# First batch's attention scores from float32 words of K and Q, V loaded behind them, and a new order of the work

## The chip, the cores and the metric

One core of one Trainium2 chip runs the kernel. The metric is device microseconds of one execution, from the first to the last instruction and what lies around them. Engines are named as in the profile: PE is TensorE (PEld its weight loads), DVE is VectorE, ACT is ScalarE, POOL is GpSimd, SP issues the DMAs.

## What is computed

Attention over 4 batches of 8 heads with 576 positions of 64 numbers, in which only scores within `tau` of the row's maximum count, and behind it two feed-forward stages (512 to 2048 to 512) on the 2304 rows that result:

```python
scores = (q @ k.T) / 8
scores = where(scores >= max(scores) - tau, scores, -1e9)
attn = exp(scores - max(scores)); attn /= sum(attn) + 1e-9
x = attn @ v                       # 2304 x 512
h = x @ w_in;  x = (h * tanh(softplus(h))) @ w_out
h = x @ w2_in; out = (h * clip(h + 3, 0, 6) / 6) @ w2_out
```

Inputs and output are float32.

## The kernel before

**Stages.** Attention comes first, and the first product of stage one (`inner`, `gemm1`, line 661) is laid into its gaps. Then come the second product of stage one (`gemm2`, line 825) and both products of stage two (lines 661 and 837). Weights are converted from float32 pairs to two float16 parts each (`convert`, lines 387 to 529); the first matrix is converted during the first batch.

**Attention.** A batch has 4 pairs of heads. A pair has 4 query tiles of 128 positions, each with two heads, and one joined tail tile that holds the last 64 positions of both heads, so 9 head tiles; a batch has 36 and all have 144. For a head tile `scores` (line 1058) fills one of two score buffers in PSUM. Then come the maximum (`peak`, line 1067, DVE), the threshold (line 1072, ACT), the exponential (line 1077, ACT), the mask (line 1080, DVE), the rounding to float16 (line 1085, ACT), its remainder (line 330, `p_ph`, POOL), a DMA transpose of both heads (line 1093, SP) and the product with V (line 1106, PE). V is scaled by one factor a batch, which needs the maxima of all four V blocks (line 937), and is split into a float16 part and a remainder (lines 1013 and 1016).

**K and Q.** The score of a float32 pair is made of rounded parts. The host stacks each transposed head twice, so K and Q have 128 partitions, of which the lower 64 repeat the upper. `pair` loads both (`rk`, `rq`, line 1000, one buffer each). K is scaled and rounded to `kd` on ACT (line 992) and its remainder goes to `kld` on DVE (line 995). Q is rounded to `qs` on ACT (line 985), and on half of the partitions the remainder of Q takes the place of the rounded value, in two subtractions, one for each head (`q_lo`, line 330 with the tile `qs`, POOL or DVE). One product over 128 partitions then adds two of the four partial products, and the two products with `kd` and `kld` give all:

```python
terms = [(st, kd.tile[:, j]), (st, kld.tile[:, j])]
for half in range(2):
    for m, (lh, rh) in enumerate(terms):
        mm(s[j].tile[:, half, :HALF], lh, rh[:, half * HALF : (half + 1) * HALF], ...)
```

That is 4 matmuls of 288 columns for a head, 8 for the tail, 40 for a pair.

**What sets the order.** A planner (`Plan`) lays the work out when the program is built. Each piece has costs by engine, a due time (from a clock of 2.55 us a head tile, with offsets by kind) and buffers; the planner always takes the piece with the earliest start, and among near ones the earliest due. The constants at the top of the file are its costs and due times. On the chip each engine runs its list in that order and waits on semaphores, so a late operand holds back all that stands behind it. `PIECE` is the number of matmuls of line 661 in one piece (4), `MOE_LAG` how late these are due, and `CONV_STEP` the spacing of the weight conversions.

Of the kernel before, what the change touches and what calls it, by code (L numbers as in the profile page):

```python
# [8 lines left out]
F32 = mybir.dt.float32  # L9
F32R = mybir.dt.float32r  # L10
# [11 lines left out]
P = 128  # L22
# [20 lines left out]
START = 7.2  # L43
PV_OFF = 6.17
PREP_AHEAD = 2.45
CONV_STEP = 1.5
CONV_AT = 3.0
LATE_STEP = 4.0
OUT_STEP = 1.5
OUT_AT = 0.0  # L50
V_AHEAD = 4.0
MOE_OFF = 9.75
MOE_LAG = 8.26
RATE = 1.32
NX = 3
FLIP = 1.61
ALPHA = {"act": 3.07, "pe": 10.98}
FITS = 0.09
# [10 lines left out]
VECTOR = 0.17  # L69
PIECE = 4  # L70
LAG = 4
# [4 lines left out]
NBLK_EARLY = 2 * B - 1  # L76
EASE = {"mk": -1.41, "ph": 1.68, "pl": -3.92, "tr": -1.06, "ex": 0.6, "s": -3.68, "th": -5.15}
# [4 lines left out]
WINDOW = {"pe": 0.05, "dve": 0.05, "act": 0.02, "pool": 0.15, "sp": 0.22}  # L82

# [201 lines left out]
def fused_kernel(ctx: ExitStack, tc, q, k, v, tau, w1i, w1o, w2i, w2o, out):  # L285
# [40 lines left out]
    def ring(name, pool, count, shape, dtype=F32):  # L326
        return Ring(name, maker(pool, name, shape, dtype), count)
# [351 lines left out]
    def inner(blk, early, at=None, gap=0.0):  # L679
# [19 lines left out]
        for fp in range(NG):  # L699
# [14 lines left out]
            if fp % 2:  # L714

                def put(e, he=he, fp=fp):
                    nc.sync.dma_start(out=hd[blk][:, fp // 2], in_=he.tile)

                h_stored[blk, fp // 2] = task(
                    {"sp": 0.5}, put, taken, [he], f"s{fp}", 2.0, fp + VECTOR  # L720
                )
# [183 lines left out]
    r_xts = ring("xts", ap, 1, [P, TAIL])  # L905
    vts, xtail, qts = [], [], []
    for i in range(4):
        pool = ap if i < 2 else ep
        qt = pool.tile([P, 2, QW], F32R, name=f"qs{i}")
        nc.gpsimd.memset(qt[:, 0, S:].bitcast(F32), 0.0)  # L910
        qts.append(qt)
# [7 lines left out]
    r_qs = [Ring("qs", lambda i, name, k=k: qts[2 * k + i], 2) for k in range(2)]  # L919
    r_vh = [Ring("vh", lambda i, name, k=k: vts[2 * k + i], 2) for k in range(2)]  # L920
# [5 lines left out]
    def batch_values(b, begin):  # L926
# [44 lines left out]
    def pair(n, begin, values, sets):  # L971
        b, hp = n // NPAIR, n % NPAIR
        base = START + begin * STEP
        early = base - PREP_AHEAD * STEP
# [4 lines left out]
        rq, rk = Buf(r_rq), Buf(r_rk)
        qs, kd, kld = Buf(r_qs[sets]), Buf(r_kd[sets]), Buf(r_kld[sets])  # L980
        vbs, vs, scaled = values
# [23 lines left out]
        ql = []
        kh = prep({"act": 1.2}, k_hi, [lk], [rk, kd], "kh")
        a = prep({"act": 1.155}, lambda e: q_hi(slice(0, 2)), [lq], [rq, qs], "qh")
        for j in range(2):
            ql.append(prep(both(S), lambda e, j=j: q_lo(e, j), [a], [rq, qs], f"ql{j}_"))
        kl = prep({"dve": 1.42}, k_lo, [kh], [rk, kd, kld], "kl")  # L1010

# [14 lines left out]
        def query_tiles(t, c, o, i):  # L1026
# [118 lines left out]
            for js in whole(MERGE_LO):  # L1145
# [262 lines left out]
```

## Time and profile before

| | |
|---|---|
| Median of 3 runs | 1089.45 us (1085.86 to 1089.76) |
| The profiled execution, its own time | 1089.44 us |
| Its span | 1087.7 us |
| PE busy | 968.7 us, 89% |
| PEld busy | 784.4 us, 72% |
| DVE busy | 604.3 us, 56% |
| ACT busy | 605.1 us, 56% |
| POOL busy | 469.2 us, 43% |
| Mean granted TensorE clock | 0.958 |

The shares are means over stages with different limits: DVE, ACT and POOL do most of their work in the first 700 us, and PE is close to full only behind the first 500. The chain of work that ended last gives PE 71% and DMA 11%, of which the transposes are 9%.

### The profile page before, as it was taken

The numbers are of one execution on the slowest core, as the hardware profiler recorded it, in microseconds if no ns is written. First come the engines' busy times: TensorE is split into PE (matmuls) and PEld (weight loads), VectorE is DVE, ScalarE is ACT, GpSimd is POOL, SyncE is SP. The second block draws the span as 40 slices with busy tenths as digits, with TensorE's granted clock in tenths as the row PEclk, the third lists the DMA queues.
The fourth block names the chain that finished last, engine by engine and source line by source line (L and its number), as shares of the span: only waits on it lengthen the run. The fifth ranks groups of instructions, "written<-read, shape, count | busy, mean of one in ns | idle before, by whom it ended". The sixth has DMA issues, their size and how long they took to land.

```text
span 1087.7 us, 21597 instructions
## 1 busy us (share of the span) xinstructions
PE 968.7 (89%) x8839; PEld 784.4 (72%) x8839; DVE 604.3 (56%) x1068; ACT 605.1 (56%) x982; POOL 469.2 (43%) x408
## 2 busy tenths in 40 slices
PE   2447688898999986979999999999999999999997
PEld 1436577787899875868888888886666667666663
DVE  7778997777787779757679678621211111111110
ACT  6637777787788778546676559522322322223322
POOL 3859766466565658634433025512222222222221
PEclk9856789998999998999999999999999999999999
DMA  6867679999999898966576967410100100100001
GB/s 258 209 172 175 139 191 238 221 229 252 195 219 218 179 227 171 239 236 235 192 233 231 335 230 265 140 40 1 58 29 11 40 30 11 40 20 20 20 1 39
DMA packets 199394, 162.87 MB, mean 150 GB/s; under 512 B 174080, under 2 KB 174080, under 8 KB 194176
## 3 DMA queue, kind: packets, MB, share of 16 engines
q1 hardware_dynamic: 199296, 161.51, 55.7%
q8 instruction: 69, 1.13, 0.4%
q14 instruction: 29, 0.24, 0.1%
HBM read 90.18 MB, written 28.84 MB: 109 GB/s over the span
## 4 chain that ended last, share of the span: by engine, by line
PE 71%; DMA 11%; DVE 8%; POOL 4%; ACT 3%; issue 2%; SPq 0%; ACTq 0%; POOLq 0%; DVEq 0%
PE h_g L661 19%; PE y_y L825 17%; PE y_y L837 17%; DMA pt_tr<-p_ph 9%; PE hp_g L661 9%; PE s_s L1058 4%; PE aux_pv L1106 4%; DVE e_ex L1080 2%; POOL p_ph L330 2%; DVE nm_pk L1067 1%; POOL qs L330 1%; DMA v_lv<-in_v 1%; ACT e_ex L1077 1%; DMA rq_lq<-in_q 1%; DMA raw_lr<-in_moe_w_in 1%
## 5 line engine op out<-in xcount | busy, mean ns | idle before, releaser
L661 PEld LDWEIGHTS <-w 128*128 128x128 f16 x3456 | 333.5, 98 | 66.9 <-issue 5.8
L330 POOL TENSOR_TENSOR p_ph<-e_ex,p_ph 128x128 f16<-128x128 f32 (+3 forms) x160 | 195.2, 1242 | 110.3 <-ACT p_ph L1085 69.0
L330 POOL TENSOR_TENSOR gs_h<-hl_r,gs_h 128x512 f16<-128x512 f32 x72 | 83.5, 1159 | 286.2 <-ACT gs_h L800 286.2
L837 PE MATMUL y_y<-w,gs_h 128*128 128x512 f16 x864 | 201.7, 379 | 0.0
L825 PE MATMUL y_y<-gs_h,w 128*128 128x256 f16 x1728 | 191.7, 273 | 0.0
L661 PE MATMUL h_g<-x_fl,w 128*128 128x256 f16 x1536 | 187.6, 275 | 3.2 <-ACT he_t L709 2.4
L825 PEld LDWEIGHTS <-w 128*128 128x128 f16 x1728 | 168.4, 98 | 19.3
L837 PEld LDWEIGHTS <-gs_h 128*128 128x128 f16 x864 | 84.5, 98 | 82.0
L800 ACT ACTIVATE gs_h<-hl_r 128x512 f16<-128x512 f32 x72 | 45.3, 629 | 172.0 <-PE y_y L837 155.4
L1067 DVE TENSOR_REDUCE nm_pk<-s_s 128x1 f32<-128x576 f32 x144 | 105.8, 751 | 35.3 <-PE s_s L1058 34.4
L1080 DVE SCALAR_TENSOR_TENSOR e_ex<-s_s,thr_th,e_ex 128x576 f32<-128x576 f32 x144 | 111.6, 810 | 15.0 <-ACT thr_th L1072 11.1
L1106 PE MATMUL aux_pv<-vh,pt_tr 128*128 128x65 f16 (+1 forms) x1296 | 91.1, 207 | 29.8 <-DMA pt_tr<-p_ph 28.1
L1077 ACT ACTIVATE e_ex<-s_s,nm_pk 128x576 f32<-128x576 f32 x144 | 104.1, 732 | 18.4 <-DVE nm_pk L1067 16.3
L784 DVE SCALAR_TENSOR_TENSOR hl_r<-hl_r,f,h_g 128x512 f32<-128x512 f32 x36 | 26.9, 747 | 156.2 <-ACT hl_r L778 156.2
L1106 PEld LDWEIGHTS <-pt_tr 128*128 128x128 f16 x2016 | 83.8, 105 | 37.6 <-DMA pt_tr<-p_ph 33.3
L1085 ACT ACTIVATE p_ph<-e_ex 128x576 f16<-128x576 f32 x144 | 95.6, 680 | 25.7 <-DVE e_ex L1080 18.6
L784 DVE SCALAR_TENSOR_TENSOR hl_r<-hl_r,f,hp_g 128x512 f32<-128x512 f32 x36 | 26.9, 746 | 145.3 <-ACT hl_r L778 145.3
L661 PE MATMUL h_g<-xl_x,w 128*128 128x256 f16 x864 | 104.3, 273 | 0.0
L661 PE MATMUL hp_g<-xl_x,w 128*128 128x256 f16 x864 | 103.0, 273 | 0.0
L1058 PE MATMUL s_s<-kda_kh,qs 128*128 128x288 f32 x200 | 68.5, 357 | 26.8 <-DVE e_ex L1080 18.3
L1058 PEld LDWEIGHTS s_s<-kda_kh,qs 128*128 128x128 f32 x200 | 43.2, 216 | 37.0 <-POOL qs L330 14.9
L804 DVE SCALAR_TENSOR_TENSOR gs_h<-hp_e,fscales,gs_h 128x512 f16<-128x512 f32 x72 | 52.6, 744 | 25.8 <-ACT gs_h L798 25.6
(321 smaller groups left out, 1297.0 us busy)
## 6 DMA issues: line engine op xcount, KB each, us to landing
hd<-he_t SPq DMA_DIRECT2D x36, 512.0 KB, 3.3
hl_l<-hd SPq DMA_DIRECT2D x36, 512.0 KB, 4.5
raw_lr<-in_moe_w_in SPq DMA_DIRECT2D x16, 1024.0 KB, 5.5
raw_lr<-in_moe_w_out SPq DMA_DIRECT2D x16, 1024.0 KB, 6.6
rk_lk<-in_k SPq DMA_DIRECT2D x16, 576.0 KB, 5.2
rq_lq<-in_q SPq DMA_DIRECT2D x16, 576.0 KB, 5.1
raw_lw<-in_moe_w_out SPq DMA_DIRECT2D x8, 1024.0 KB, 7.3
v_lv<-in_v SPq DMA_DIRECT2D x16, 320.0 KB, 4.6
```

What stands on the lines that cost most here:

```text
L330: engine[e].tensor_tensor(dst, a, b, ALU.subtract)
L661: mm(hv[:, j, :], wj[:, wl, c * P : (c + 1) * P], x.tile[:, c, xl, :], start=j == 0 and n == 0, stop=j == 1 and n == 11, skip_group_check= ...
L784: nc.vector.scalar_tensor_tensor(half(g), half(g), wsc[2]["f"][:, fp : fp + 1], h.tile, ALU.min, ALU.mult)
L804: nc.vector.scalar_tensor_tensor(s.tile[:, 1], gv(), fs[:, fp : fp + 1], s.tile[:, 0], ALU.mult, ALU.subtract)
L825: mm(yv[:, h, :], wt[m2][f // 2][:, f % 2, wl, c * P : (c + 1) * P], gs[fp].tile[:, gl, f % 2, :], start=fp == 0 and n == 0, stop=fp == NG ...
L837: mm(y.tile[:, j], gs[fp].tile[:, gl, f % 2, j * P : (j + 1) * P], wt[m2][f // 2][:, f % 2, wl, :], start=fp == 0 and n == 0, stop=fp == N ...
L1058: mm(s[j].tile[:, half, :HALF], lh, rh[:, half * HALF : (half + 1) * HALF], start=m == 0, stop=m == len(terms) - 1,)
L1067: nc.vector.tensor_reduce(neg.tile[:, j : j + 1], sv(j), AX.XY, ALU.max, negate=True)
L1077: nc.scalar.activation(ev(j), sv(j), AF.Exp, bias=neg.tile[:, j : j + 1])
L1080: nc.vector.scalar_tensor_tensor(ev(j), sv(j), thr.tile[:, j : j + 1], ev(j), ALU.is_ge, ALU.mult)
L1085: nc.scalar.activation(p16.tile[:, js, :S], e_.tile[:, js], AF.Copy)
L1106: mm(ov[:, dst, :d], pt.tile[:, j, ch, :], part.tile[:, src, vc, :], start=i == j == ch == 0 and part is vh, stop=j == w - 1 and ch == 8, ...
```

## The change

For the batches below `DIRECT`, that is for the first alone, K and Q are no longer split. The upper 64 partitions of each, thus each word once, are loaded straight into the buffers `kd` and `qs` (no `rk`, `rq`, `kld`), ACT scales K in place, and the scores are float32 matmuls over 64 partitions: 2 for a head, 4 for the tail, 20 for a pair. The loads of the first batch may start earlier (`DIRECT_AHEAD`), and its V is due later (`V_FIRST`), behind K and Q of two pairs. The zeros behind `qs` are now filled for each pair on POOL (`pad`) and not once for each buffer. The planner's constants are new, so the whole order is: of its costs and due times the diff shows those that are spoken of later.

```diff
-CONV_STEP = 1.5
+CONV_STEP = 2.06
-MOE_LAG = 8.26
+MOE_LAG = 15.8
-PIECE = 4
+PIECE = 2
...
+        first = START + (begin - V_FIRST) * STEP if b == 0 else at
-            a = task({"sp": 0.5}, load, [], [vb], f"lv{i}_", 0.91, 0.0, [prev[5]])
+            a = task({"sp": 0.5}, load, [], [vb], f"lv{i}_", 0.91, first - at, [prev[5]])
...
+        direct = b < DIRECT
-        early = base - PREP_AHEAD * STEP
+        early = base - (DIRECT_AHEAD if direct else PREP_AHEAD) * STEP
...
+        def words(t):
+            return t.tile[:D, :, :S].bitcast(F32)
+
+        def load_words_of(dst, src):
+            return lambda e: nc.sync.dma_start(out=words(dst), in_=src[n][:D])
+
+        def k_scaled(e):
+            nc.scalar.activation(words(kd), words(kd), AF.Copy, scale=qscale[:D])
+
+        def pad(e):
+            nc.gpsimd.memset(qs.tile[:, 0, S:].bitcast(F32), 0.0)
+
+        padded = prep({"pool": 0.16}, pad, [], [qs], "qp")
+        if direct:
+            lk = prep({"sp": 0.5}, load_words_of(kd, k), [], [kd], "lk", 0.82, order=[prev[4]])
+            lq = prep({"sp": 0.5}, load_words_of(qs, q), [], [qs], "lq", 0.82, order=[lk])
+            kl = prep({"act": 1.2}, k_scaled, [lk], [kd], "kh")
+            ql = [lq, lq]
+        else:
...
+                if direct:
+                    qt, ks = qs.tile[:D].bitcast(F32), [kd.tile[:D].bitcast(F32)]
+                else:
+                    qt, ks = qs.tile, [kd.tile, kld.tile]
                 if c < NQ:
                     q0 = j * TAIL + c * P
-                    st = qs.tile[:, j, q0 : q0 + P]
-                    terms = [(st, kd.tile[:, j]), (st, kld.tile[:, j])]
+                    terms = [(qt[:, j, q0 : q0 + P], k[:, j]) for k in ks]
```

In the new order the matmuls of line 661 are laid out differently against the head tiles. Ahead of the 37th, the 73rd and the 109th head tile's scores there stood 84, 544 and 916 of them, and 1256 ahead of the last product with V; now there stand 48, 466, 822 and 1270. The order itself is shown at three places.

The start of SP's list of DMAs, before and then changed (`lv` is V, `lk` and `lq` are K and Q, `lr` is a block of weights):

```order
L954 DMA v_lv_0_0_163<-in_v 128x640
L954 DMA v_lv_0_0_165<-in_v 128x640
L954 DMA v_lv_0_0_167<-in_v 128x640
L954 DMA v_lv_0_0_169<-in_v 128x640
L1000 DMA rk_lk_0_171<-in_k 128x1152
L1000 DMA rq_lq_0_173<-in_q 128x1152
L450 DMA raw_lr_0_0_175<-in_moe_w_in 128x1024
L450 DMA raw_lr_1_0_177<-in_moe_w_in 128x1024
L1000 DMA rk_lk_0_202<-in_k 128x1152
```

```order
L1011 DMA kda_lk_0_159<-in_k 64x1152
L1011 DMA qsa_qp_0_155<-in_q 64x2x576
L1011 DMA kda_lk_0_166<-in_k 64x1152
L1011 DMA qsa_qp_0_157<-in_q 64x2x576
L957 DMA v_lv_0_0_169<-in_v 128x640
L957 DMA v_lv_0_0_171<-in_v 128x640
L957 DMA v_lv_0_0_173<-in_v 128x640
L957 DMA v_lv_0_0_175<-in_v 128x640
L1011 DMA kdb_lk_0_178<-in_k 64x1152
L1011 DMA qsb_qp_0_161<-in_q 64x2x576
L455 DMA raw_lr_0_0_181<-in_moe_w_in 128x1024
```

The four V blocks stood first and one pair's K and Q behind them. Now K and Q of two pairs, on 64 partitions, stand first, V behind them, and K and Q of the other two pairs next.

DVE's list from its first V maximum to its first masks, before and then changed (`vm` is a V maximum, `kl` a K remainder, `vl` a V remainder, `top` a weight maximum, `pk` a score maximum, `e_ex` a mask):

```order
L937 TENSOR_REDUCE vt_vm_0_1_179<-v_lv_0_0_167 128x1
L937 TENSOR_REDUCE vt_vm_0_1_179<-v_lv_0_0_169 128x1
L942 TENSOR_REDUCE vs_ve_1_184<-vt_vm_0_1_179 128x1
...
L995 SCALAR_TENSOR_TENSOR klda_kl_2_197<-rk_lk_0_171,qscale,kda_kh_1_189 128x1152
L1016 SCALAR_TENSOR_TENSOR vla_vl_3_205<-v_lv_0_0_163,vs_ve_1_184,vh_128 128x640
L387 TENSOR_REDUCE top_146<-raw_lr_0_0_175 128x1
L1067 TENSOR_REDUCE nm_pk_0_0_1_218<-s_s_0_0_0_208 128x1
...
L1016 SCALAR_TENSOR_TENSOR vla_vl_3_230<-v_lv_0_0_165,vs_ve_1_184,vh_132 128x640
L1067 TENSOR_REDUCE nm_pk_0_0_1_218<-s_s_0_1_0_220 128x1
L387 TENSOR_REDUCE top_146<-raw_lr_1_0_177 128x1
L1080 SCALAR_TENSOR_TENSOR e_ex_0_0_2_228<-s_s_0_0_0_208,thr_th_0_0_1_240,e_ex_0_0_2_228 128x576
```

```order
L939 TENSOR_REDUCE vt_vm_0_1_195<-v_lv_0_0_169 128x1
L1094 TENSOR_REDUCE nm_pk_0_0_1_201<-s_s_0_0_0_183 128x1
L939 TENSOR_REDUCE vt_vm_0_1_195<-v_lv_0_0_171 128x1
L939 TENSOR_REDUCE vt_vm_0_1_195<-v_lv_0_0_173 128x1
L939 TENSOR_REDUCE vt_vm_0_1_195<-v_lv_0_0_175 128x1
L1094 TENSOR_REDUCE nm_pk_0_0_1_201<-s_s_0_1_0_192 128x1
L944 TENSOR_REDUCE vs_ve_1_210<-vt_vm_0_1_195 128x1
L945 TENSOR_SCALAR vs_ve_1_210<-vs_ve_1_210 128x1
L1107 SCALAR_TENSOR_TENSOR e_ex_0_0_2_204<-s_s_0_0_0_183,thr_th_0_0_1_213,e_ex_0_0_2_204 128x576
```

The first score maximum stood behind all V maxima, the V scale, a K remainder and a V remainder; now it stands behind one V maximum, and the second score maximum stands behind all four.

POOL's list from its first work on the first batch, before and then changed (`qs` is a subtraction into Q, `p_ph` the remainder of the probabilities, `cvt` and `w` are steps of the weight conversion):

```order
L330 TENSOR_TENSOR qs_126<-rq_lq_0_173,qs_126 64x576 x2
L330 TENSOR_TENSOR qs_130<-rq_lq_0_225,qs_130 64x576
L330 TENSOR_TENSOR p_ph_0_0_1_247<-e_ex_0_0_2_228,p_ph_0_0_1_247 128x2x64
L330 TENSOR_TENSOR p_ph_0_0_1_247<-e_ex_0_0_2_228,p_ph_0_0_1_247 128x2x512
L330 TENSOR_TENSOR qs_130<-rq_lq_0_225,qs_130 64x576
L330 TENSOR_TENSOR p_ph_1_0_1_290<-e_ex_1_0_2_269,p_ph_1_0_1_290 128x2x64
L330 TENSOR_TENSOR p_ph_1_0_1_290<-e_ex_1_0_2_269,p_ph_1_0_1_290 128x2x512
L511 TENSOR_TENSOR cvt_c_0__1_281<-cvt_c_0__1_281,eight 128x512 x2
```

```order
L335 TENSOR_TENSOR p_ph_0_0_1_220<-e_ex_0_0_2_204,p_ph_0_0_1_220 128x2x64
L335 TENSOR_TENSOR p_ph_0_0_1_220<-e_ex_0_0_2_204,p_ph_0_0_1_220 128x2x512
L335 TENSOR_TENSOR p_ph_1_0_1_263<-e_ex_1_0_2_241,p_ph_1_0_1_263 128x2x64
L335 TENSOR_TENSOR p_ph_1_0_1_263<-e_ex_1_0_2_241,p_ph_1_0_1_263 128x2x512
L516 TENSOR_TENSOR cvt_c_0__1_288<-cvt_c_0__1_288,eight 128x512 x2
L335 TENSOR_TENSOR p_ph_0_0_1_335<-e_ex_0_0_2_286,p_ph_0_0_1_335 128x2x64
```

The subtractions into `qs` stood among the remainders of the probabilities; in the first batch there are none now, and the list goes from one `p_ph` to the next with only weight steps between.

## Rows read from the trace of the kernel before

**Rows 1.** Windows: stretch, length, busy PE PEld DVE ACT POOL, clock, DMA share, GB/s
```profile
0.00:14.90 14.90, 1.59 (x5) 1.09 (x5) 8.92 (x20) 6.88 (x8) 4.50 (x18) 1.00 0.84 317
14.90:148.50 133.60, 77.05 (x663) 65.89 (x664) 115.23 (x195) 86.36 (x140) 94.59 (x77) 0.74 0.68 174
148.50:253.80 105.30, 93.74 (x1179) 85.74 (x1178) 80.25 (x139) 82.72 (x148) 67.38 (x54) 1.00 1.08 229
253.80:347.00 93.20, 87.94 (x1083) 80.84 (x1081) 73.76 (x134) 76.77 (x141) 55.17 (x47) 0.96 1.03 218
347.00:455.00 108.00, 89.48 (x1103) 80.33 (x1102) 85.19 (x157) 80.94 (x144) 72.61 (x60) 0.95 0.93 199
...
500.00:1087.70 587.70, 581.68 (x4493) 438.67 (x4491) 211.63 (x362) 247.74 (x368) 155.37 (x138) 1.00 0.29 99
```

**Rows 2.** Windows, score maxima alone (line 1067), DVE busy (count)
```profile
14.90:148.50 133.60, 26.34 (x36) 0.74 0.68 174
148.50:253.80 105.30, 26.13 (x37) 1.00 1.08 229
```

**Rows 3.** Windows, first products of the stages alone (line 661), PE, PEld (count)
```profile
14.90:148.50 133.60, 11.99 (x86) 8.67 (x87) 0.74 0.68 174
148.50:253.80 105.30, 55.75 (x460) 42.66 (x458) 1.00 1.08 229
...
347.00:455.00 108.00, 41.36 (x341) 31.56 (x340) 0.95 0.93 199
```

**Rows 4.** Timeline of the opening: start us, us, engine, line
```profile
5.06 1.61 DVE L937 TENSOR_REDUCE vt_vm<-v_lv 128x1 f32<-128x640 f32 x2 [0.40 <-DMA v_lv<-in_v]
6.90 1.60 DVE L937 TENSOR_REDUCE vt_vm<-v_lv 128x1 f32<-128x640 f32 x2 [0.22 <-DMA v_lv<-in_v]
...
13.30 0.61 PE L1058 MATMUL s_s<-kda_kh,qs 128*128 128x288 f32 x1 [3.60 <-POOL qs L330]
...
16.65 0.76 DVE L1067 TENSOR_REDUCE nm_pk<-s_s 128x1 f32<-128x576 f32 x1
...
18.45 1.53 DVE L1080 SCALAR_TENSOR_TENSOR e_ex<-s_s,thr_th,e_ex 128x576 f32<-128x576 f32 x2
```

**Rows 5.** Waits of the first 150 us: us in total, times, longest
```profile
PE s_s L1058 <- POOL qs L330: 7.0, 4, 3.6
...
DVE nm_pk L1067 <- PE s_s L1058: 5.7, 10, 1.6
...
PE s_s L1058 <- DVE kldb_kl L995: 3.3, 1, 3.3
```

**Rows 6.** Lines by form: count, busy us, mean ns, idle before
```profile
L995 DVE SCALAR_TENSOR_TENSOR klda_kl<-rk_lk,qscale,kda_kh 128x1152 fp32r<-128x1152 f32 x10 | 14.3, 1427 | 0.3 <-ACT kda_kh L992 0.3
...
L992 ACT ACTIVATE kda_kh<-rk_lk,qscale 128x1152 fp32r<-128x1152 f32 x10 | 12.5, 1248 | 0.3 <-PE s_s L1058 0.2
...
L330 POOL TENSOR_TENSOR qs<-rq_lq,qs 64x576 fp32r<-64x576 f32 x32 | 46.9, 1466 | 27.5 <-ACT qs L985 26.2
```

**Rows 7.** Windows: score maxima at 40 us, all engines at the batch's end
```profile
40.00:70.00 30.00, 3.01 (x4) 0.67 0.70 178
...
100.00:148.50 48.50, 35.26 (x322) 30.19 (x319) 44.60 (x76) 33.79 (x61) 34.90 (x31) 0.79 0.64 157
```

**Rows 8.** Timeline, score matmuls at the half and the full clock
```profile
48.44 0.44 PE L1058 MATMUL s_s<-kldb_kl,qs 128*128 128x288 f32 x1
...
49.88 0.44 PE L1058 MATMUL s_s<-kldb_kl,qs 128*128 128x288 f32 x1
...
209.63 0.30 PE L1058 MATMUL s_s<-klda_kl,qs 128*128 128x288 f32 x1
...
210.96 0.29 PE L1058 MATMUL s_s<-klda_kl,qs 128*128 128x288 f32 x1
```

**Rows 9.** Float32 matmuls of lines 1227 and 1221: duration ns, min, median, max
```profile
L1227 PE MATMUL aux_fl<-istack,xtail x32: 217/275/323, 116.0 to 456.4; 128*128 128x64 f32 x32
...
L1221 PE MATMUL aux_fl<-ident,xn_dn x64: 270/273/474, 39.5 to 453.7; 128*128 128x128 f32 x64
```

More of the change, by code (lines that the diff above doesn't have):

```diff
@@ L43 @@
 START = 7.2
-PV_OFF = 6.17
+PV_OFF = 3.72
+V_FIRST = 1.0
+DIRECT_AHEAD = 8.0
+DIRECT = 1
 PREP_AHEAD = 2.45
-CONV_STEP = 1.5
+CONV_STEP = 2.06
 CONV_AT = 3.0
-LATE_STEP = 4.0
-OUT_STEP = 1.5
+LATE_STEP = 2.61
+OUT_STEP = 2.39
 OUT_AT = 0.0
-V_AHEAD = 4.0
+V_AHEAD = 6.29
 MOE_OFF = 9.75
-MOE_LAG = 8.26
+MOE_LAG = 15.8
 RATE = 1.32
@@ L56 @@
 FLIP = 1.61
[L57 removed]
+ALPHA = {"act": 3.07, "pe": 6.71}
 FITS = 0.09
@@ L69 @@
 VECTOR = 0.17
-PIECE = 4
+PIECE = 2
+TR_DMA = 1.22
+HD_DMA = 1.6
 LAG = 4
@@ L719, in inner @@
                 h_stored[blk, fp // 2] = task(
-                    {"sp": 0.5}, put, taken, [he], f"s{fp}", 2.0, fp + VECTOR
+                    {"sp": 0.5}, put, taken, [he], f"s{fp}", HD_DMA, fp + VECTOR
                 )
@@ L890, in fused_kernel @@
     r_rk = ring("rk", ap, 1, [P, 2, S])
+    r_qs = [ring("qs" + "ab"[k], (ap, ep)[k], 2, [P, 2, QW], F32R) for k in range(2)]
     r_kd = [ring("kd" + "ab"[k], (ap, ep)[k], 2, [P, 2, S], F32R) for k in range(2)]
@@ L905, in fused_kernel @@
     r_xts = ring("xts", ap, 1, [P, TAIL])
-    vts, xtail, qts = [], [], []
+    vts, xtail = [], []
     for i in range(4):
         pool = ap if i < 2 else ep
-        qt = pool.tile([P, 2, QW], F32R, name=f"qs{i}")
-        nc.gpsimd.memset(qt[:, 0, S:].bitcast(F32), 0.0)
-        qts.append(qt)
         vt = pool.tile([P, 2, NQ + 1, D + 1], F16, name=f"vh{i}")
@@ L973, in pair @@
         base = START + begin * STEP
[L974 removed]
+        direct = b < DIRECT
+        early = base - (DIRECT_AHEAD if direct else PREP_AHEAD) * STEP
         def prep(engines, fn, deps, bufs, tag, dma=0.0, at=early, order=()):
             return add(engines, fn, deps, bufs, at, 0.0, dma, f"{tag}{n}", order)
[L979 to L980 removed]
+        qs, kd = Buf(r_qs[sets]), Buf(r_kd[sets])
+        if not direct:
+            rq, rk, kld = Buf(r_rq), Buf(r_rk), Buf(r_kld[sets])
         vbs, vs, scaled = values
@@ L1000, in load @@
             return lambda e: nc.sync.dma_start(out=dst.tile, in_=src[n])
-        lk = prep({"sp": 0.5}, load(rk, k), [], [rk], "lk", 1.64, order=[prev[4]])
-        lq = prep({"sp": 0.5}, load(rq, q), [], [rq], "lq", 1.64, order=[lk])
-        prev[4] = lq
[L1005 to L1010, printed above, removed]
+        def words(t):
[13 more added lines that the diff above has]
+        else:
+            lk = prep({"sp": 0.5}, load(rk, k), [], [rk], "lk", 1.64, order=[prev[4]])
+            lq = prep({"sp": 0.5}, load(rq, q), [], [rq], "lq", 1.64, order=[lk])
+            ql = []
+            kh = prep({"act": 1.2}, k_hi, [lk], [rk, kd], "kh")
+            a = prep({"act": 1.155}, lambda e: q_hi(slice(0, 2)), [lq], [rq, qs], "qh")
+            for j in range(2):
+                ql.append(prep(both(S), lambda e, j=j: q_lo(e, j), [a], [rq, qs], f"ql{j}_"))
+            kl = prep({"dve": 1.42}, k_lo, [kh], [rk, kd, kld], "kl")
+        prev[4] = lq
         def v_hi(e):
@@ L1044, in scores @@
             def scores(j):
+                if direct:
+                    qt, ks = qs.tile[:D].bitcast(F32), [kd.tile[:D].bitcast(F32)]
+                else:
+                    qt, ks = qs.tile, [kd.tile, kld.tile]
                 if c < NQ:
                     q0 = j * TAIL + c * P
-                    st = qs.tile[:, j, q0 : q0 + P]
-                    terms = [(st, kd.tile[:, j]), (st, kld.tile[:, j])]
+                    terms = [(qt[:, j, q0 : q0 + P], k[:, j]) for k in ks]
                 else:
-                    flat = qs.tile.rearrange("p a n -> p (a n)")
+                    flat = qt.rearrange("p a n -> p (a n)")
                     terms = [
-                        (flat[:, q0 : q0 + P], k.tile[:, jj])
+                        (flat[:, q0 : q0 + P], k[:, jj])
                         for jj, q0 in enumerate((FULL, S))
-                        for k in (kd, kld)
+                        for k in ks
                     ]
@@ L1116, in query_tiles @@
             for j in heads:
-                deps = [ql[j], kl] if c < NQ else [*ql, kl]
-                held = [s[j], qs, kd, kld]
+                deps = [ql[j], kl] if c < NQ else [*ql, kl, padded]
+                held = [s[j], qs, kd] if direct else [s[j], qs, kd, kld]
+                cost = (0.56, 0.96) if c < NQ else (1.08, 1.92)
                 a = go(
-                    {"pe": 0.56 if c < NQ else 1.08}, lambda e, j=j: scores(j), deps + [prev[0]],
+                    {"pe": cost[direct]}, lambda e, j=j: scores(j), deps + [prev[0]],
                     held, "s", j,
```

7 lines of the change are left out of this document (3 added, 4 removed).

## The prediction

> **What bounds the kernel now.** I read the busy time by stretch first [rows 1]. From 500 us to the end TensorE is busy 581.68 of 587.70 us, with the clock at 1.00: that stage is pure matrix work and its length is the work that is left over. Everything before it is attention, with the first product of the expert stage (line 661) pushed into TensorE's gaps; there no engine is full. So the end of the kernel is the time at which attention is over plus the matrix work not yet done by then. The sums below are therefore about the length of attention, and about matmuls that move across its end.
>
> Within attention the first batch stands out. The row maxima (line 1067) number 36 a batch, one for each tile of one head (and one for each joined tail) [rows 2]: the first 36 take 133.60 us, 3.71 us each, and the next 37 take 105.30 us, 2.85 each. In those 133.60 us VectorE is busy 115.23 us (86%), TensorE only 77.05 at a mean clock of 0.74 [rows 1]. So the first batch is VectorE's, with holes; the later batches are TensorE's (93.74 of 105.30 and 87.94 of 93.20 us), except the last, where it is busy 89.48 of 108.00 us. The matmuls of line 661 number 86 in the first of these stretches, 460 in the second and 341 in the last [rows 3]: the last batch has too few to fill its gaps.
>
> Then the opening [rows 4]: VectorE reduces V from 5.06 us on, but the first score waits until 13.30 us for GpSimd's subtraction into `qs`, and the first mask is at 18.45 us. Last, the waits of the first 150 us [rows 5].
>
> **The change part by part.** The sum is made against the profiled execution's 1089.44 us (span 1087.7), which is also the median of the runs, 1089.45.
>
> *The opening: −4 us, between −7 and 0.* K and Q of two pairs (four loads of 288 KB) now stand ahead of V on SP's queue. The first K can be there when V's first block is now, 5.06 us [rows 4]; the scaling on ScalarE is 1.25 us [rows 6], taken as the same on half the partitions since each still has 1152 words, so the first score can start at about 6.4 us, 6.9 earlier than 13.30. But VectorE's second maximum is now queued behind all four V maxima, and the last V comes 1.18 MB later, 3.7 us at the 317 GB/s of the opening [rows 1]. The fourth V maximum ends today at 6.90 + 1.60 = 8.50 [rows 4], then at 12.2; the second score maximum would end near 13.0 instead of 16.65 + 0.76 = 17.41. On ScalarE the threshold now stands behind the scaling of the third pair's K, whose load comes after all of V; that eats part of the 4.4. I take 4, with 7 if V does not matter and 0 if the loads are slower than that.
>
> The Trainium skill speaks against this term: "SBUF — State Buffer", section "Door 1: The DMA port swizzle", says that a transfer to partitions 0 to 63 reaches only half of the memory's ports, so these loads would run at half rate. No load of the kernel before goes to 64 partitions alone, so the trace cannot show it. By it the 3.7 us would be 7.4, the opening would gain about 0.3 us, and the sum would be 1081.7.
>
> *VectorE's work in the first batch: −5 us, between −5 and 0.* The four K remainders of the first batch go, 1.43 us each [rows 6]. By the order, ahead of the 36th maximum five of these become two (those of the second batch's first pairs), and one V maximum comes in for one conversion step that goes out: 3 x 1.43 = 4.3 us less of 115.23. At the same share of 86% that is 5.0 us of time.
>
> *Waits for the preparation: −5 us, between −15 and 0.* Eight GpSimd subtractions of 1.47 us [rows 6], 11.7 us, leave the first batch; TensorE's scores wait 7.0 us for them and 3.3 us for a K remainder there [rows 5], of which 3.6 belong to the opening. That leaves 6.7; I count 5, since VectorE is what is late next. The upper end is the slowest piece: 4 maxima in the 30 us from 40 to 70 us [rows 7], which at 3.71 each would be 15 us. Four ScalarE roundings of Q also go (as large as the scalings of K, 1.25 us [rows 6]), and 2.4 MB of loads; both are costed at nothing, because ScalarE (86.36 of 133.60) and the DMA engines (0.68) are not what the batch waits for [rows 1]. GpSimd gets 12 more fills of the padding, short ones, on an engine with 39 us free in that stretch alone.
>
> *TensorE's longer scores: +6 us, between 0 and +38.* 160 matmuls on the rounded pairs become 80 on float32 words. The old ones follow each other every 0.133 us at the full clock (from 209.63 to 210.96 eleven of them) and every 0.24 at the half (from 48.44 to 49.88 seven; there the spacing shows the level, not the clock column) [rows 8]. For float32 the nearest rows are the tail's product, 32 matmuls for its 16 calls, thus two for one, and the flips; 217 ns at 64 columns against 270 at 128 [rows 9] gives 0.83 ns a column, so 288 columns in two passes cost 0.48 us. Forty score products a pair become twenty: 160 x 0.133 = 21.3 us becomes 80 x 0.48 = 38.4, +17 us at the full clock; at the half clock (38.4 to about 76) +38. If a pass cost no more than an old matmul it would be +0. TensorE has 56 us free in this batch, so most is hidden, but a tile's first score is ahead of its maximum. VectorE waited for a score 10 times in 150 us, 5.7 us in all [rows 5]. Those ten grow by 0.4 to 0.95 us (a head's four old matmuls against two new, at either clock), I say 6 us. If every tile were late by it, all 38 count.
>
> *The rest of the order: −4.5 us, between −8 and +6.* By the new order the matmuls of line 661 ahead of the 37th, 73rd and 109th score tile are 48, 466 and 822, and 1270 ahead of the last attention product; before they were 84, 544, 916 and 1256. So the second and third batch, where TensorE is nearly full, lose 42 + 16 matmuls, and the last one gains 108. At 0.11 us each (41.36 / 341 is 0.12 [rows 3], in records that overlap a little) that is 6.4 us out of full stretches and 12 us into one with 18.5 us free. I count −3, since the 12 do not all fit; the worst is +6. The 14 more by the end of attention leave 1.5 us less behind it. That the pieces are 2 matmuls and not 4 lets a score in 0.2 us sooner; nothing is counted for it.
>
> Sum: −4 − 5 − 5 + 6 − 4.5 = −12.5; I round to −12 and forecast **1077.5 us**.
>
> **The rivals.** *The clock comes up and the first batch closes ranks.* TensorE's clock was mostly at the lower of its two levels (1.2 of 2.4 GHz) there, 0.74 on the mean; longer products fill TensorE's idle time. If it stays at the upper one, the +6 goes, and VectorE could reach the share that it has at the end of this batch, 44.60 of 48.50 us, 92% [rows 7]: (115.23 − 4.3) / 0.92 = 120.6 instead of 133.6, −13. With −4 for the opening, −6 and −1.5 for the order it is −24.5, **1065 us**. The Trainium skill, "TensorE: Matmul & The Clock Gate", section "What's actually happening", states that activity releases the throttle, which would make this rival likelier. Against it: VectorE's holes at 40 to 70 us also come from transposes and weight conversions that stay.
>
> *No difference.* The opening brings 1 us (slow loads), the waits nothing since the weight conversions stand there anyway, the new distribution nothing: −1 − 5 + 6 − 1.5 is −1.5, **1088 us**. For it: the 64 partitions, and the transposes' place in the chain of waits.
>
> *Slower: the long scores set the pace.* There are two score buffers, both of one tile, so the next tile cannot start before the masks. If the clock stays low and VectorE then has nothing else to do, each tile is later by its added matrix time, 38 us in all; with the other terms (−4 − 5 − 5 − 4.5) it is +19.5, **1109 us**. It decides once the added time on the path passes 18.5 us, half of the 38, that is, once VectorE waits for about half of the tiles and not for 10 of 36. Against it: the two passes over the scores are 26.34 us [rows 2] and 36 x 0.77 = 27.7 us (a pair of masks is 1.53 [rows 4]) of VectorE's 115.23, so half of its work in this batch is other work that can stand in the wait.
>
> That the change does not do what it says is excluded by the order: 640 score matmuls became 480 and 80.
>
> **How the numbers follow.** A measurement of this kernel tells about 0.5%, 5.4 us, from no change. The forecast case (1070 to 1084) has 0.46, the clock rival (1055 to 1070) 0.23, no difference 0.18, slower 0.13. That is faster 0.69, same 0.18, slower 0.13. The range of 8 in 10 runs from 1058, inside the clock rival, to 1093, past no difference; the slower case is left out, with the best end of the clock rival.
>
> **What would show it.** Right: the first score at 6 to 7 us and the first mask near 14; the 37th maximum at 136 to 142 us instead of 148.5; float32 matmuls in pairs, 0.24 us apart each at the full clock; no GpSimd `qs` rows before the second batch's pairs; TensorE's busy time from the third quarter on unchanged, and the last batch nearer to full. The clock rival shows in a mean clock near 1 in the first batch and its end before 132 us. Wrong: VectorE's idle time behind scores well over 15 us in the first batch, or a first mask as late as now, or the second and third batch longer than 105 and 93 us.

## The result and the profile after

The changed kernel takes 1072.0 us, the median of 4 runs (1068.35 to 1073.61), against 1088.4 (1085.86 to 1089.76) for the kernel before: ratio 0.9848, 95% interval 0.9815 to 0.9880. The forecast was 1077.5, with a range from 1058 to 1093. The profiled execution took 1073.61 us.

The page gives the busy time of each engine:

```profile
span 1071.8 us, 21567 instructions
...
PE 1007.3 (94%) x8839; PEld 794.4 (74%) x8839; DVE 593.3 (55%) x1060; ACT 599.7 (56%) x982; POOL 451.8 (42%) x412
```

TensorE is busy 38.6 us longer than before (968.7), in a span 15.9 us shorter: its idle time fell from 119.0 to 64.5 us. Where, the windows say (length, busy PE PEld DVE ACT POOL, clock, DMA share, GB/s; cut at the 1st, 37th, 73rd and 109th row maximum and at the last product with V, as [rows 1]):

```profile
0.00:10.80 10.80, 4.03 (x8) 2.50 (x8) 1.49 (x8) 3.79 (x3) 1.52 (x16) 1.00 0.78 195
10.80:150.40 139.60, 113.34 (x688) 79.18 (x688) 114.81 (x209) 88.66 (x143) 88.82 (x76) 0.78 0.73 183
150.40:243.80 93.40, 87.52 (x1075) 77.78 (x1073) 77.77 (x133) 78.24 (x143) 59.01 (x53) 1.00 0.99 224
243.80:333.20 89.40, 84.98 (x1022) 76.36 (x1021) 73.13 (x126) 74.05 (x139) 54.63 (x50) 0.96 1.07 224
333.20:441.20 108.00, 100.80 (x1259) 90.00 (x1256) 84.65 (x158) 84.66 (x156) 74.49 (x65) 0.98 1.03 215
484.00:1071.80 587.80, 580.66 (x4481) 437.42 (x4479) 212.26 (x362) 247.64 (x367) 157.49 (x140) 1.00 0.29 101
```

The first batch is over at 150.4 us, 1.9 later than before: nothing is gained there. Inside it a gain comes and goes: the 13th maximum starts at 54.5 us instead of 70.3, and the 24 tiles from there to the 37th maximum take 96.1 us instead of 78.4. The second batch is 11.9 us shorter (93.40 against 105.30) and the third 3.8. The fourth has the same length, 108.00, with TensorE busy 100.80 us of it instead of 89.48. The stage behind is unchanged.

The first products (line 666, PE and PEld) show what moved, beside [rows 3]:

```profile
10.80:150.40 139.60, 9.08 (x69) 7.12 (x70) 0.78 0.73 183
150.40:243.80 93.40, 49.29 (x400) 36.74 (x397) 1.00 0.99 224
...
333.20:441.20 108.00, 55.20 (x452) 42.06 (x453) 0.98 1.03 215
```

The second batch has 400 of them instead of 460, the fourth 452 instead of 341.

The timeline of the opening, beside [rows 4]:

```profile
5.34 1.25 ACT L1014 ACTIVATE kda_lk<-kda_lk,qscale 64x1152 f32<-64x1152 f32 x1 [3.33 <-DMA kda_lk<-in_k]
...
6.77 4.18 PE L1085 MATMUL s_s<-kda_lk,qsa_qp 64*128 64x288 f32 x8 [6.77 <-DMA qsa_qp<-in_q]
...
10.12 0.82 DVE L939 TENSOR_REDUCE vt_vm<-v_lv 128x1 f32<-128x640 f32 x1 [5.82 <-DMA v_lv<-in_v]
...
13.70 0.74 DVE L1094 TENSOR_REDUCE nm_pk<-s_s 128x1 f32<-128x576 f32 x1
...
15.62 1.54 DVE L1107 SCALAR_TENSOR_TENSOR e_ex<-s_s,thr_th,e_ex 128x576 f32<-128x576 f32 x2 [0.93 <-ACT thr_th L1099]
```

The first score starts 6.5 us earlier (6.77 for 13.30), the first mask only 2.8 (15.62 for 18.45).

The score products of the first batch by stretch (line 1085, PE and PEld, clock), and two groups of eight on the timeline:

```profile
66.00:69.40 3.40, 2.47 (x8) 1.34 (x8) 1.00 1.09 193
69.40:93.30 23.90, 12.53 (x24) 7.49 (x24) 0.50 0.63 162
93.30:110.30 17.00, 6.58 (x24) 4.25 (x24) 1.00 0.69 132
110.30:147.90 37.60, 22.20 (x44) 13.48 (x44) 0.50 0.71 171
```

```profile
99.47 2.20 PE L1085 MATMUL s_s<-kda_lk,qsa_qp 64*128 64x288 f32 x8
134.71 4.21 PE L1085 MATMUL s_s<-kdb_lk,qsb_qp 64*128 64x288 f32 x8 [0.72 <-DVE e_ex L1107]
```

A group of eight is one score tile for both heads, two records for a call. It takes 2.20 us at the upper level of the clock (2.4 GHz) and 4.21 at the lower; before, eight old matmuls 0.24 us apart took 1.9 us even at the lower [rows 8]. Only 32 of the 160 records of this batch stand at the upper level. The trace has no record of the clock before 66.0 us (in the kernel before, 43.4 us), and there the column says 1.00; but eight score records from 52.16 us take 4.17 us, the spacing of the lower level. So the means 0.74 and 0.78 of the first batch are both too high. From 66 us on the clock of both kernels is recorded, and it is lower than before, not higher (before, then changed):

```profile
66.00:148.50 82.50, 52.43 (x443) 44.81 (x444) 75.02 (x133) 55.51 (x94) 59.53 (x51) 0.69 0.65 166
```

```profile
66.00:150.40 84.40, 72.21 (x462) 51.72 (x460) 69.33 (x129) 53.65 (x87) 59.50 (x52) 0.64 0.69 163
```

And the waits of the first 150 us, beside [rows 5]:

```profile
DVE nm_pk L1094 <- PE s_s L1085: 15.2, 17, 2.1
...
PE s_s L1085 <- DVE e_ex L1107: 10.9, 8, 5.6
```

VectorE now waits 15.2 us for scores, in 17 times, where it was 5.7 in 10.

### The profile page after: what moved, and what is told of

It reads as the page before. It is cut to its first block, busy times and chain, and to the rows that moved or that the text cites. A ratio compares the mean times of both kernels' runs of the same rounds, so it can differ in the third digit from the quotient of the medians.

```text
span 1071.8 us, 21567 instructions
## 1 busy us (share of the span) xinstructions
PE 1007.3 (94%) x8839; PEld 794.4 (74%) x8839; DVE 593.3 (55%) x1060; ACT 599.7 (56%) x982; POOL 451.8 (42%) x412
## 4 chain that ended last, share of the span: by engine, by line
PE 52%; DVE 2%; DMA 1%; ACT 0%; issue 0%; ACTq 0%
PE y_y L842 17%; PE y_y L830 16%; PE h_g L666 10%; PE hp_g L666 9%; DMA raw_lr<-in_moe_w_in 1%; DVE gs_h L809 0%; ACT he_t L714 0%; DVE top L392 0%; DVE cvt_c__1_8276 L524 0%; DVE cvt_c__1_8355 L524 0%; DVE cvt_c__1_8355 L529 0%; DVE cvt_c__1_8276 L529 0%; DVE sm_zmy L556 0%; DVE col L392 0%; ACT gs_h L803 0%; ACT hp_e L775 0%
## 5 line engine op out<-in xcount | busy, mean ns | idle before, releaser
L335 POOL TENSOR_TENSOR p_ph<-e_ex,p_ph 128x128 f16<-128x128 f32 (+3 forms) x160 | 190.9, 1215 | 105.3 <-ACT p_ph L1112 80.5
L1133 PE MATMUL aux_pv<-vh,pt_tr 128*128 128x65 f16 (+1 forms) x1296 | 93.1, 209 | 17.2 <-DMA pt_tr<-p_ph 16.5
L809 DVE SCALAR_TENSOR_TENSOR gs_h<-hp_e,fscales,gs_h 128x512 f16<-128x512 f32 x72 | 53.0, 744 | 19.1 <-ACT gs_h L803 18.9
L803 ACT ACTIVATE gs_h<-hp_e,fscales 128x512 f16<-128x512 f32 x72 | 48.4, 682 | 23.9 <-PE y_y L830 19.3
L775 ACT ACTIVATE hp_e<-hl_l 128x512 f32<-128x512 f32 x72 | 42.1, 594 | 21.8 <-DVE gs_h L809 13.0
```

Of the source, the lines that this page charges most:

```text
L335: engine[e].tensor_tensor(dst, a, b, ALU.subtract)
L803: nc.scalar.activation(s.tile[:, 0], gv(), AF.Copy, scale=fs[:, fp : fp + 1])
L809: nc.vector.scalar_tensor_tensor(s.tile[:, 1], gv(), fs[:, fp : fp + 1], s.tile[:, 0], ALU.mult, ALU.subtract)
L1133: mm(ov[:, dst, :d], pt.tile[:, j, ch, :], part.tile[:, src, vc, :], start=i == j == ch == 0 and part is vh, stop=j == w - 1 and ch == 8, ...
```

## The experiments

Twelve kernels, each timed in three rounds beside the kernel before. The table has, from each profiled execution: the 37th maximum, the last product with V, what lies behind that, and TensorE's idle time (stretch less its matmul records) in the second to fourth batch; then the time against before, from the ratio of the runs times 1088. A profiled execution can stand up to 6 us off its median (E10 and E12 do), so differences of a few us between rows of the trace of two kernels are not read.

| | 37th maximum | last V product | behind | idle, batches 2 to 4 | time against before |
|---|---|---|---|---|---|
| before | 148.7 | 454.5 | 633.1 | 35.4 | |
| after | 150.6 | 440.8 | 631.0 | 17.5 | -16.5 |
| E1 new order, old scores | 148.8 | 449.6 | 638.8 | 24.7 | -0.3 |
| E2 old order, new scores | 153.1 | 462.3 | 633.0 | 32.1 | +7.0 |
| E3 cheap scores | 137.8 | 426.7 | 627.4 | 16.4 | -30.4 |
| E4 old lag and piece | 154.3 | 452.1 | 636.9 | 30.2 | +3.7 |
| E5 nearly free preparation | 145.2 | 450.5 | 631.8 | 34.0 | -4.2 |
| E6 old piece | 147.9 | 441.1 | 643.3 | 22.9 | -5.4 |
| E7 old lag | 155.5 | 453.3 | 639.9 | 25.8 | +4.5 |
| E8 lag 17.0 | 148.3 | 436.5 | 631.3 | 17.9 | -17.4 |
| E9 two pairs | 142.9 | 437.3 | 643.9 | 21.2 | -6.0 |
| E10 three pairs | 153.8 | 457.9 | 634.1 | 27.3 | +9.0 |
| E11 V first | 154.4 | 446.4 | 638.9 | 22.0 | -1.6 |
| E12 before, lag 9.5 | 146.8 | 452.3 | 630.8 | 34.9 | +1.5 |

**E1 and E2: each half of the change alone.** E1 is the changed kernel with the old scores, E2 the new scores with the constants of before.

```diff
-DIRECT = 1
+DIRECT = 0          # E1; E2 keeps 1 and has PV_OFF, CONV_STEP, LATE_STEP, OUT_STEP, V_AHEAD,
                     # MOE_LAG, ALPHA, PIECE, EASE, WINDOW and the two DMA costs of before
```

> The changed kernel's planner constants, but K and Q of the first batch split as before (DIRECT = 0); the computation is whole. Theory A (the gain lies in the new order behind the first batch, where 103 of its 144 maxima gained about 14 us, and the float32 scores pay nothing in the first batch): about as fast as the changed kernel, 1068 to 1078 us. Theory B (the float32 scores are what pays, since they free VectorE, GpSimd and ScalarE): the gain goes, 1083 us or more. Between them, 1079 to 1082, both have a share.

> The other half: float32 scores in the first batch, early loads of K and Q and V behind them, with the planner constants of the kernel before; the computation is whole. Theory A: no gain, 1083 to 1095 us, and a first batch that ends later than at 148 us. Theory B: most of the gain, 1070 to 1078 us.

E1: 1088.5 us, ratio 0.9997 (0.9980 to 1.0014). E2: 1095.1 us, ratio 1.0064 (1.0045 to 1.0083). E1 came as theory B had it and E2 about as theory A had it, so each theory fell in the other run. Neither half gains; together they gain 16.5. So no sum of one part's worth and the other's describes this change.

**E3: the length of the products.** The order is the changed one on every engine; the first batch's scores use only the upper 16 bits of the words, as bfloat16.

```diff
-qt, ks = qs.tile[:D].bitcast(F32), [kd.tile[:D].bitcast(F32)]
+qt, ks = tops(qs), [tops(kd)]     # tile[:D].bitcast(BF16), every second number
```

> The changed kernel in its own order, but the first batch's score matmuls read only the upper 16 bits of each word, as bfloat16, so they take one pass and the scores of that batch are rounded. It prices the length of the float32 products alone. If their length is on the path of the first batch (score matmuls there busy 77.6 us against 42.8 before): the 37th maximum comes 8 us or more earlier than at 150.6 us, and the time is 1060 to 1066 us. If it is hidden as the prediction had it (6 us): 1066 to 1069 us. If wholly hidden: 1070 to 1073.

1058.2 us, ratio 0.9721 (0.9703 to 0.9738), 13.8 us below the changed kernel. Its first batch, cut the same way, and VectorE's wait for scores in it:

```profile
10.80:137.70 126.90, 64.45 (x607) 43.36 (x608) 115.12 (x210) 87.67 (x144) 88.87 (x76) 0.77 0.79 202
```

```profile
DVE nm_pk L1097 <- PE s_s L1088: 0.9, 3, 0.4
```

With short products the batch is 12.7 us shorter and VectorE is busy 115.12 of 126.90 us, 91%: the batch is VectorE's again. The wait for scores falls from 15.2 to 0.9 us. So the length of the float32 products costs 13 to 14 us, more than the 10.9 us that the first batch saves elsewhere (148.7 to 137.8 at the 37th maximum).

The length is not all that the later tiles lose. In E3 the 24 tiles from the 13th to the 37th maximum still take 85.4 us, 7.0 more than before. In E3 and in the changed kernel the 36th maximum stands behind steps of the weight conversion on VectorE's list; it comes 11.5 and 10.5 us after the 35th, where it came 3.8 us after it in the kernel before.

**E4, E6, E7, E8: the two constants of the expert pieces.** Each is the changed kernel with `PIECE` or `MOE_LAG` alone or both put back, or the lag nudged on.

```diff
-MOE_LAG = 15.8
-PIECE = 2
+MOE_LAG = 8.26      # E4, E7; E8 has 17.0
+PIECE = 4           # E4, E6
```

> The changed kernel with the two constants of the first expert product put back, PIECE = 4 and MOE_LAG = 8.26, so that 544, 888 and 1252 of these matmuls stand ahead of the 73rd and 109th head tile and the last attention product (466, 822 and 1270 in the changed kernel); the computation is whole. If the finer pieces and the later distribution bring the gain behind the first batch: 1080 to 1087 us, with 37th to 73rd maximum at about 105 us again. If they do not: 1070 to 1076 us.

> The changed kernel with its expert pieces put back to 4 matmuls, all else as changed. Both constants together gave 1091.8. Theory D (the distribution of the first-product matmuls over the batches decides): here 48, 488, 844 and 1252 stand ahead of the 37th, 73rd and 109th maximum and of the last product with V, 22 more in the full stretches and 40 fewer in the last batch, so about +3 to +5, near 1076. Theory L (the length of a piece decides, since a score stands behind a whole piece on TensorE's queue): most of the 20 us comes back, 1086 or more.

> The changed kernel with the lag of the expert pieces put back to 8.26, pieces of 2 kept. Theory D (distribution): 48, 518, 850 and 1252, so 52 more in the second batch, 18 fewer in the last: +6 to +10, near 1080. Theory L (length of a piece): within 4 us of 1072, since the pieces stay short. If neither constant alone gives half of the 20 us, the two work only together.

> The changed kernel with the lag of the expert pieces moved a little on, from 15.8 to 17.0: 48, 476, 832 and 1270 matmuls of the first product ahead of the four marks, against 48, 466, 822 and 1270. Theory D (distribution): within 3 us of 1072. Theory S (the fine place of single pieces decides, so that any nudge of a constant throws the time about): off by more than 6 us, with single tiles that stall 8 us or more in other places than now.

E4: 1091.8, ratio 1.0034 (1.0015 to 1.0052). E6: 1084.6, 0.9950 (0.9928 to 0.9973). E7: 1092.4, 1.0041 (1.0019 to 1.0063). E8: 1071.4, 0.9840 (0.9808 to 0.9872). The lag alone is worth 21 us and the piece alone 11, against 20 for both together. E4's second batch takes 101.5 us, not the 105 of its first theory. Theory D gave 4 and 8 for E6 and E7, so the counts of matmuls alone do not set the time; theory L fell with E7, whose pieces stay short. E6's attention ends when the changed kernel's does (441.1 and 440.8), and its loss lies behind. There the second product waits for VectorE. E6's longest waits (us in total, times, longest), and the windows from 560 to 580 us of E6 and then of the changed kernel:

```profile
PE y_y L830 <- DVE yl_zhy L570: 4.3, 1, 4.3
PE h_zp L366 <- ACT he_t L714: 3.1, 1, 3.1
PE hp_g L666 <- DVE hl_r L789: 2.2, 1, 2.2
```

```profile
560.00:580.00 20.00, 15.74 (x123) 12.92 (x121) 16.59 (x41) 11.19 (x18) 4.99 (x5) 0.83 0.80 288
```

```profile
560.00:580.00 20.00, 18.85 (x174) 16.76 (x172) 19.13 (x43) 10.86 (x17) 6.54 (x6) 1.00 0.63 219
```

A wait of 4.3 us, and the clock falls during it: 123 matmuls in 20 us instead of 174, which is 5.9 us of work. The other two waits shown are followed by a lower clock as well. In all, up to its last matmul, TensorE is idle 12.7 us behind attention in E6 and 8.2 in the changed kernel; it works at the lower level for 11.7 us in E6 and not at all in the changed kernel; and it has 18 more matmuls to do. That is 4.5, 5.8 and about 2 us, which makes up the 12 us. E7 loses mostly in its second batch, 13 us longer,

```profile
155.40:262.00 106.60, 96.97 (x1092) 85.83 (x1091) 83.49 (x137) 80.97 (x143) 64.01 (x54) 0.96 0.92 225
```

and 5 us in its first and 9 behind attention, while its third and fourth together are 6 us shorter. E8 moves nothing: this nudge does not throw the changed order.

**E5: what the removed preparation was worth.** The kernel before, in its own order; in the first batch the remainders of Q and K cover one column, and the rounded K is read a second time in place of its remainder.

```diff
-sub(e, qs.tile[r, j, :S], rq.tile[r, j], qs.tile[r, j, :S].bitcast(F32))
+n = 1 if b == 0 else S
+sub(e, qs.tile[r, j, :n], rq.tile[r, j, :n], qs.tile[r, j, :n].bitcast(F32))
...
```

> The kernel before, in its own order, with the first batch's preparation made nearly free: the remainders of Q and K are computed on one column only and the low K product reads the rounded K a second time, so the score values of the first batch are not the reference's; every instruction stays in its place. Theory P (the prediction's two terms for VectorE's first-batch work and for the waits for preparation, -5 and -5): the 37th maximum comes near 139 us instead of 148.7 and the time is near 1079. Theory Q (tiles 20 to 36 are held by TensorE's in-order queue behind pieces of line 661 and transposes, not by the preparation): the 37th maximum stays at 146 to 150 and the time within 4 us of 1089.

1085.3 us, ratio 0.9961 (0.9938 to 0.9985), so 4.2 us (1.6 to 6.7) less. Theory Q holds but for the 37th maximum, at 145.2 a little ahead of its bound. Most of the gain lies in the opening: the 9th maximum is at 38.7 us instead of 41.6, the 37th 3.4 us earlier. The slow piece of the batch stays: tiles 9 to 12 take 27.0 us, against 28.6 before. The waits from 38 to 70 us say why:

```profile
PE aux_fl L1224 <- DVE top L398: 6.9, 1, 6.9
...
PE aux_pv L1109 <- DMA pt_tr<-p_ph: 4.5, 2, 4.3
```

TensorE's list has flips of finished rows and products with V ahead of these scores, and it waits for those; the first of the two waits shown was 4.2 us before. A quicker preparation does not change the list. With the new scores these four tiles take 12.0 us in E2 and 13.3 in the changed kernel; they take 21.4 us in E1, which has the old scores in the new order, and 20.9 in E9, where their pair is prepared as before. So what went was the preparation's place in the plan, more than its duration.

**E9 and E10: fewer pairs with float32 scores.**

```diff
-direct = b < DIRECT
+direct = n < 2      # E10: n < 3
```

> The changed kernel with float32 scores for the first two pairs only (up to tile 18); the third and fourth pair are prepared and multiplied as before. 48, 436, 790 and 1248 matmuls of line 666 stand ahead of the four marks. Theory F (float32 products pay where the clock is at half, which is mostly in the third and fourth pair; the preparation that comes back is cheap): the 37th maximum near 144 us instead of 150.6, about -8 for the products and +2 for the preparation, -6 in all: 1066. Theory S (the constants fit this one order, and any other that is planned with them falls back): 1080 or more, with stalls of single tiles in batches 2 to 4.

> The changed kernel with float32 scores for the first three pairs, the fourth as before (48, 434, 844 and 1282 matmuls of line 666 ahead of the marks). Theory F: about half of what two pairs give, -3, 1069, with tiles 27 to 36 shorter than the 45 us they take now. Theory S: 1080 or more.

One thing in these expectations was wrong: a batch runs the first four tiles of each pair in turn and then the last five of each, so the first two pairs are tiles 1 to 8 and 17 to 26. Nor is the clock low mostly in the third and fourth pair: by the spacing of the score records in the changed kernel all tiles up to 62 us have the lower level too. E9: 1082.8 us, ratio 0.9945 (0.9922 to 0.9967). Its first batch does what theory F said (142.9, forecast 144):

```profile
10.90:142.90 132.00, 90.61 (x670) 68.77 (x670) 110.19 (x194) 88.15 (x144) 87.91 (x76) 0.83 0.74 187
...
560.00:580.00 20.00, 15.73 (x129) 13.22 (x128) 15.62 (x38) 10.02 (x16) 3.21 (x3) 0.91 0.77 280
```

From the 28th to the 37th maximum it takes 30.7 us, the changed kernel 42.7. But its second to fourth batch are 4 us longer than those of the changed kernel, and behind attention it loses 13, with the same wait of 4.3 us as E6. So its time is not theory F's 1066 but lies where theory S had it. E10: 1099.4 us, ratio 1.0083 (1.0051 to 1.0114); the end of its first batch stalls (tiles 33 to 36 take 29.2 us, 18.9 in the changed kernel), so F failed here in the first batch too, and S held for the time.

**E11: V first again.**

```diff
-V_FIRST = 1.0
+V_FIRST = 9.0
```

> The changed kernel with V's four loads ahead of those of K and Q again, all else as changed (the order behind is planned anew: 48, 400, 754 and 1208 matmuls of line 666 ahead of the marks). By the prediction's opening term: the first score about 3.7 us later (near 10.5), the first mask near 16 to 17 instead of 15.6, the 9th maximum later by 1 to 3 us; by the rival that the loads of 64 partitions run at half rate and V behind them costs as much as it brings, the 9th maximum at the same time as now, 41.2. The total moves by that and by the 62 matmuls more behind attention's end (+6 if attention does not get shorter by as much): 1074 to 1081.

1087.0 us, ratio 0.9985 (0.9965 to 1.0006). The first score starts at 10.82 us and the 9th maximum comes at 43.9 instead of 41.2, as the opening term said. The first mask, at 20.43 us, is 4 us later than was said, and the time misses its 1074 to 1081. The rest of the 15 us is the order planned anew behind it: second batch 101.0 us instead of 93.4, and 8 us more behind attention.

**E12: a nudge of the kernel before.**

```diff
-MOE_LAG = 8.26
+MOE_LAG = 9.5
```

> The kernel before with one constant moved a little, the lag of the expert pieces from 8.26 to 9.5, to see how far a small shift of the plan throws the time of that kernel (76, 532, 908 and 1272 matmuls of line 661 ahead of the marks). If an order's time is mostly the place of single pieces, it lands 6 us or more from 1088; if it is set by the shares of work, within 3 us.

1091.1 us, ratio 1.0014 (0.9993 to 1.0035): within 3 us, as for E8. One small nudge of this lag did not throw the time about at either point; larger moves of one constant of the changed kernel (E6, E7, E11) cost 11 to 21 us.

## Why the prediction was right, and where its steps were not

The sum was right in sign and near in size, -12 for -16.5, and its frame held for this pair: what lies behind attention is 633.1 and 631.0 us, so nearly all of the gain is attention's length. (It does not hold for every order: in E6, E7, E9 and E11 that part is 8 to 13 us longer.) The terms inside were not right, and that the sum came out near is luck in good part.

*Opening (-4).* The first score came at 6.77 us (6 to 7 was said), the first mask at 15.62 (14). The second maximum ends at 14.44 instead of 17.41, 3.0 us earlier where 4.4 was worked out. By the 9th maximum 0.4 us is left of it, 41.2 against 41.6. One reason is that V comes later than was counted. This is the traffic of the first 20 us in half-microseconds, of the changed kernel and of E11, where V on 128 partitions goes first:

```profile
DMA  0000086999999999999999999999988999999999
GB/s 0 0 0 0 0 120 221 332 212 212 230 212 217 180 203 221 221 205 348 415 410 410 415 449 290 189 203 243 247 234 344 442 410 419 339 235 184 189 238 264
```

```profile
DMA  0000675699999999999999999989999599989999
GB/s 0 0 0 0 31 57 51 230 399 410 410 384 399 449 291 226 207 212 240 184 217 203 203 217 203 249 171 175 210 260 252 131 377 377 442 370 365 203 203 189
```

With the DMA engines equally busy, K and Q move at about 212 GB/s and V at about 410. In the kernel before, where K and Q come on 128 partitions behind V, there is no such drop:

```profile
7.00:9.50 2.50, 0.07 (x1) 0.00 (x0) 1.81 (x4) 0.52 (x2) 0.00 (x0) 1.00 1.03 421
```

So V's first maximum starts at 10.12 instead of 5.06 us and its fourth ends at 13.78 instead of 8.50, 5.3 later; 3.7 was counted. The Trainium skill, "SBUF — State Buffer", section "Door 1: The DMA port swizzle", says half rate for such loads; the trace agrees (212 / 410 is 0.52). The estimate that the prediction worked out from it does not come out: 7.4 us for V and 0.3 for the opening, since it doubled a time that went by 317 GB/s, the mean of a stretch with idle DMA time; 1.18 MB at 212 GB/s are 5.6 us. That 0.4 us is left at the 9th maximum, a later place, is no sign for it. (Its sum is off as well: with -0.3 for -4 the terms give 1080.6 and not 1081.7.) What takes the rest between the second and the 9th maximum was not separated. The length of the products does not, since E3 has its 9th maximum at 41.05 us. E11 shows that V ahead would cost 2.7 us.

*VectorE's work and the waits for preparation (-5 and -5).* E5 prices the two at -4.2 and not -10: "Waits for the preparation: −5 us" counted waits as time gained, and in E5 other entries of TensorE's list fill that time. A larger saving is seen only where the preparation is gone from the lists. E3 against before has all that the first batch saves apart from the length of the products: 148.7 to 137.8, -10.9 for the -14 of the three terms. That holds 36 fewer matmuls of the expert stage ahead of the 37th maximum too (48 for 84), which no term counted.

*Longer scores (+6).* This term was half of what it should have been. TensorE's own cost was right: a call takes 0.48 us at the upper clock and 0.96 at the lower, 42.8 us of score products became 77.6, and +38 was the bound. But "Those ten grow by 0.4 to 0.95 us" took the number of late tiles as fixed. It rose from 10 to 17, and E3 measures 12.8 us at the 37th maximum, twice the term and a third of the bound. The two passes that were assumed are two records a call in the trace. The Trainium skill, "FP8 and Floating Point Precision", section "TensorE Precision Notes", counts four passes for float32. In time the trace agrees: a call takes 0.48 us where the rounded one took 0.133, 3.6 times, and 0.96 for 0.24 at the lower clock, 4 times.

*The rest of the order (-4.5).* This term was the farthest off. It gave -17.8: 15.7 in the second to fourth batch, 2.1 behind. "I count −3, since the 12 do not all fit" was wrong: they all fit. The last batch took 111 more matmuls of line 666 in the same 108.00 us, its idle time going from 18.5 to 7.2. The second and third lost 9.2 us of TensorE's work, and 6.5 us of its idle time besides, which was not counted at all.

So two errors met: the first batch gave +1.9 where -8 was forecast (-10.9 + 12.8), and the batches behind gave 13 more than forecast. They cancel by luck. The clock rival was wrong: from 66 us on the mean clock is 0.64, and the first batch does not end before 132 us. What it said of VectorE was seen, but without the longer products: 91% in E3, where 92% was assumed. The slower rival had part of the mechanism. It wanted VectorE to wait for about half of the tiles, and 17 waits in 36 tiles were found; but 12.8 us came onto the path, not the 18.5 at which it would decide. Of the signs, the 37th maximum at 136 to 142 us did not come (150.6), and the 15.2 us that VectorE waits for scores stand at the mark that was set for wrong.

What stays open is why the new order and the new scores gain only together. E1 and E2 show that they do, and E4, E6, E7, E9, E10 and E11 that the changed kernel falls back by 10 us or more when a constant or a part of the batch is set otherwise, in different places: at the end of the first batch (in E4, E7 and E10 the 37th maximum comes 14 to 16 us after the 36th, in the changed kernel 1.1), in the second batch, or behind attention. Which entry of the plan makes each of them was not separated. Nor was it tried whether the old scores would gain as much with constants tuned for them: E1 has constants that came with the new scores, and E12 moves one constant a little. So that the float32 scores are needed for the gain is shown for these two sets of constants alone. No version that computes the whole reference was clearly better than the changed kernel (E8 is the same within its interval).

## What to carry to other kernels

When work is taken out of a kernel whose order is planned, price it twice: by making it short with the order kept, and by taking it out. Here the first gave 4 us and the second changed the list. For an operation that gets longer on an engine with idle time, count how many consumers become late, not only how much later the late ones get. And tune the plan's constants again for each form of the kernel before judging that form: by either half alone this change would have been dropped.

## What the runs showed of the hardware

- TensorE was at the lower level of its clock for most of the first batch although it was busy 113.34 of 139.60 us; in the records from 110.30 to 147.90 us the clock is 0.50 while score products alone fill 22.20 of 37.60 us. More work on the engine did not bring the clock up: from 66 us on it was busy 72.21 of 84.40 us instead of 52.43 of 82.50, at a mean clock of 0.64 instead of 0.69.
- Behind attention in E6 a wait of 4.3 us cost 5.9 us of matmuls: the clock fell during it and stayed lower for the work behind it. Waits of 3.1 and 2.2 us there were followed by the lower level too.
- Loads of 288 KB to 64 partitions moved about 212 GB/s, loads of 320 KB to 128 partitions about 410, with the DMA engines equally busy.
